# Attention with a squared-ReLU MLP on one core: phases of six and eight score units around one whole product unit

## The chip, the core and the metric

The kernel runs on one core of one Trainium2 chip, as a single program. The metric is the time of one execution in microseconds (us). Engines are named as the profile names them: PE (TensorE; PEld is its weight load), DVE (VectorE), ACT (ScalarE), POOL (GpSimd) and SP (the queue that issues most DMAs). Three timed runs of the kernel before stand at 1247.25, 1248.50 and 1248.59 us, median 1248.5 us.

## The reference

For 2048 positions and width 512, with 32 heads of size 16 that share one key and one value head:

```
x = A_x;  g = sigmoid((x * gate_w).sum(-1))
a = softmax((x@wq) . (x@wk)^T / 4) @ (x@wv)  per head, then @ wo
b = relu(x @ w1 + b1)**2 @ w2 + b2           # F = 1792
out = g * a + (1 - g) * b
```

Everything is float32. Large products are made of rounded parts: a number is split into a rounded part r and a rest l, and r·r + r·l + l·r is summed.

## The kernel before, in words

**Score units.** The heads are worked in 32 groups ("its") of four heads, each with 512 query columns. A group has 32 score units: 128 keys times 256 query columns for all four heads. A unit is two matmuls of 49 rows each, one on the upper and one on the lower half of the PE array's rows, into two PSUM banks (`s`, L730). One exponential of ACT over 128x1024 elements (L734) reads both banks and writes half of an `e` tile in SBUF. There are 1024 units, two buffers of `s` (two banks each) and four `e` tiles (two units each).

**Context.** Later, units are multiplied with the values (`acc`, L745): for two units that share an `e` tile, four matmuls of 512 columns on four column strips of the array.

**Product units.** All other large products (the queries, x·w1, h·w2, the output projection) are units of 9 or 12 terms, some at the end of 3 or 6. A term has 128 rows, and is made as two matmuls of 64 rows: half 0 on the upper rows of the array, half 1 on the lower. `stream` (L188) gives each half a PSUM bank of its own (`mm`, three buffers) and lets half 1 follow half 0 five terms behind (`LAG`). The halves are added by DVE: `first` evicts one bank, `second` the other. A w1 unit (`hidden`, L624) thus takes five DVE instructions: bias (L637), add (L641), squared ReLU (L642), and the split into r and l (L178, L179). An h·w2 unit (`summed`, L646) takes two of L664.

**Phases.** PE's order is written by `phase` (L1002): scores of the coming units, with terms of product units between them (a "slot" is one term of half 0 beside one term of half 1), and then the context of units scored a phase earlier. `plan` (L1028) takes four units with eight slots (a full phase) while product work is ahead, and two units with two or three slots (a light phase) after that. The scores run four or two units ahead of the context.

**The other queues.** DVE also divides the finished contexts in pieces of 86 columns (`divide`, L752: four instructions and an accumulator read, at most one piece a phase), and makes the rests l of weights and inputs (L487, L179); `turn_of_chores` (L606) deals these out by a budget. ACT rounds weights (L491) and copies each finished group's `acc` out (L771). DMAs bring weights, store and load queries and contexts, and store `res`, the MLP's part, to DRAM.

Of the kernel before, what the change touches and what calls it, by code (L numbers as in the profile page):

```python
# [21 lines left out]
KT = D // 128  # L22
# [12 lines left out]
BUDGET = 2.7  # L35
PARTS = [slice(a, min(a + 86, CH)) for a in range(0, CH, 86)]
LANDS = 8.0
GROUPS = (0, 1, 2, 3), (4, 5, 6, 7), (8, 9, 10), (11, 12, 13)
FULL, LIGHT = 4, 2
LAG = 5  # L40
# [25 lines left out]
def exact_shift(tc, k_aug, v_ext, qs, oTs, gms, ress, cs, wo, split, outproj, stream, unpack):  # L66
# [63 lines left out]
    with tc.tile_pool(name="gx", bufs=1) as gx, tc.tile_pool(name="gy", bufs=4, space=PSUM) as gy:  # L130
# [6 lines left out]
        for c in range(NC):  # L137
            oT = gx.tile([128, KT, CH], F32, name="oT")
            orr, orl = [gx.tile([128, KT, CH], F32R, name=n) for n in ("orr", "orl")]
            before = gx.tile([128, KT, CH], F32, name="res")  # L140
            ots = [gx.tile([128, D], F32, name=f"ot{i}") for i in range(2)]
            nc.sync.dma_start(before, ress[c])
            nc.sync.dma_start(oT, oTs[c * NG:c * NG + NG].rearrange("(t u) d n -> (u d) t n", u=2))
            split(orr, orl, oT)
            for _ in stream(outproj(c, before, ots, orr, orl, wor, wol, "gm"), gy):
                pass
# [3 lines left out]
def mix_kernel(ctx: ExitStack, tc: tile.TileContext, xT, wkv, wq, wo, w12, b1, b2, cst, out):  # L150
# [37 lines left out]
    def stream(units, pp):  # L188

        late = []

        def follow(keep):
            if len(late) > keep:
                late.pop(0)()

        for unit in units:
            if unit is None:
                if late:  # L200
                    follow(0)
                    yield 1
                else:
                    yield 0
                continue
            terms, outs, tag = unit
            banks = [pp.tile([128, CH], F32, name=tag)]

            def product(i, half, terms=terms, outs=outs, banks=banks, tag=tag):
                if len(banks) == half:  # L210
                    banks.append(pp.tile([128, CH], F32, name=tag))
                a, b = terms[i]
                rows = slice(64 * half, 64 * half + 64)
                nc.tensor.matmul(banks[half], a[rows], b[rows], start=i == 0, stop=i == len(terms) - 1)  # L214
                if i == len(terms) - 1:
                    outs[half](banks[half])

            for i in range(len(terms)):
                late.append(lambda i=i, p=product: p(i, 1))
                product(i, 0)  # L220
                follow(LAG)
                yield 1
        while late:
            follow(0)
            yield 1

# [5 lines left out]
    def outproj(c, before, ots, orr, orl, wor, wol, tag):  # L232
        for j in range(4):
# [4 lines left out]
            def first(p, s=s, j=j, ot=ot):  # L238
                nc.vector.scalar_tensor_tensor(ot, p, g[:, s:s + 1], before[:, j], op0=OP.mult, op1=OP.add)
# [13 lines left out]
    with fast, tc.tile_pool(name="at", bufs=1) as at, \  # L253
# [352 lines left out]
        def turn_of_chores(slots):  # L606
# [3 lines left out]
            if soon:  # L610
                return soon.pop(0)()
# [498 lines left out]
```

## Time and profile before

| | |
|---|---|
| median of three runs | 1248.5 us |
| span of the profiled execution | 1243.9 us |
| PE busy | 1233.2 us (99%) |
| ACT busy | 1060.3 us (85%), of it 980.3 in the 1024 exponentials |
| DVE busy | 623.1 us (50%) |
| granted TensorE clock | 1.000 |

The span runs from the first to the last instruction of the profiled execution. Its own time is that span and what lies around it at launch and end; the median of the timed runs is 4.6 us above the span. A PE that is busy for 99% has work in flight all the time, since its matmuls overlap; how densely they start is read from the timeline.

### The profile page before, as it was taken

How to read it: one execution, taken by the hardware profiler on the slowest of the kernel's cores; microseconds unless marked ns; L12 is line 12 of the kernel's file. 1: busy time of each engine (PE TensorE's matmuls, PEld its weight loads, DVE VectorE, ACT ScalarE, POOL GpSimd, SP SyncE). 2: the span in 40 equal slices, each digit the busy share in tenths (PEclk: the TensorE clock that was granted, in tenths of full speed). 3: DMA queues.
4: the chain of work that ended last, by engine and by line, in shares of the span. 5: the costliest groups of instructions: out<-in, count | busy, mean ns of one | idle time of the engine just before them, and what ended most of it. 6: DMA issues, size and time to landing. Idle time of an engine off the chain costs nothing.

```text
span 1243.9 us, 24095 instructions
## 1 busy us (share of the span) xinstructions
PE 1233.2 (99%) x9839; PEld 612.5 (49%) x9839; DVE 623.1 (50%) x1246; ACT 1060.3 (85%) x1178; POOL 59.4 (5%) x75
## 2 busy tenths in 40 slices
PE   9999999999999999999999999999999999999997
PEld 4555555555555555555555555555433333343343
DVE  5666665545565542744827365355441454232433
ACT  6888888888888987988988888888899999999985
POOL 1000300000002000000200000002000000000000
PEclk9999999999999999999999999999999999999999
DMA  6334321211232210222202121121110120011101
GB/s 215 101 96 143 105 79 40 82 48 65 69 113 84 75 57 25 82 73 98 72 29 82 65 81 61 56 81 65 56 57 26 35 69 31 31 48 47 44 31 37
DMA packets 44388, 85.57 MB, mean 69 GB/s; under 512 B 10450, under 2 KB 10706, under 8 KB 43760
## 3 DMA queue, kind: packets, MB, share of 16 engines
q1 hardware_dynamic: 37024, 68.27, 17.0%
q0 software_dynamic: 7104, 15.44, 3.7%
q8 instruction: 79, 1.29, 0.4%
q14 instruction: 37, 0.30, 0.1%
q10 hardware_dynamic: 144, 0.26, 0.1%
HBM read 54.68 MB, written 20.97 MB: 61 GB/s over the span
## 4 chain that ended last, share of the span: by engine, by line
PE 96%; ACT 1%; DVE 1%; DMA 0%; issue 0%; SPq 0%; ACTq 0%
PE acc L745 38%; PE mm L214 31%; PE s L730 25%; ACT e L734 1%; PE mm L312 1%; DMA xf<-in_xT 0%; PE mm L186 0%; PE s L322 0%; DVE kmx L334 0%; PE acc L352 0%; ACT w1r L491 0%; PE mm L802 0%; DVE ot L1073 0%; DVE xlagain L179 0%; DVE w1l L487 0%
## 5 line engine op out<-in xcount | busy, mean ns | idle before, releaser
L734 ACT ACTIVATE e<-s 128x1024 f32<-128x1024 f32 x1024 | 980.3, 1023 | 153.5 <-PE s L730 152.0
L745 PE MATMUL acc<-e,v_ext 128*32 128x512 f32 (+1 forms) x4224 | 509.4, 587 | 0.0
L730 PE MATMUL s<-qa,k_aug 49*128 49x512 f32 x2048 | 452.6, 433 | 0.1
L730 PEld LDWEIGHTS s<-qa,k_aug 49*128 49x128 f32 x2048 | 193.7, 183 | 331.8 <-ACT e L734 300.2
L664 DVE SCALAR_TENSOR_TENSOR res<-mm,omg,res 128x512 f32<-128x512 f32 x128 | 95.8, 750 | 252.2 <-PE mm L214 252.2
L214 PE MATMUL mm<-w2r,hr 64*128 64x512 f32 x896 | 212.2, 393 | 1.0 <-DVE big L641 0.6
L745 PEld LDWEIGHTS acc<-e,v_ext 128*32 128x32 f32 x4224 | 102.7, 108 | 208.7 <-issue 202.0
L214 PE MATMUL mm<-w2l,hr 64*128 64x512 f32 x448 | 159.4, 393 | 0.0
L214 PEld LDWEIGHTS mm<-w2r,hr 64*128 64x128 f32 x896 | 129.0, 187 | 18.4 <-DVE res L664 1.2
L214 PEld LDWEIGHTS mm<-w2l,hr 64*128 64x128 f32 x448 | 83.4, 187 | 7.4
L214 PE MATMUL mm<-xragain,w1l 64*128 64x512 f32 x224 | 80.3, 393 | 0.0
L214 PE MATMUL mm<-xr,w1l 64*128 64x512 f32 x224 | 79.4, 393 | 0.0
L214 PE MATMUL mm<-xlagain,w1r 64*128 64x512 f32 x224 | 79.2, 392 | 0.0
L214 PE MATMUL mm<-xragain,w1r 64*128 64x512 f32 x224 | 78.7, 392 | 0.0
L214 PE MATMUL mm<-xl,w1r 64*128 64x512 f32 x224 | 78.5, 391 | 0.0
L214 PE MATMUL mm<-xr,w1r 64*128 64x512 f32 x224 | 77.0, 392 | 0.0
L641 DVE TENSOR_TENSOR big<-big,mm 128x512 f32<-128x512 f32 x56 | 38.5, 687 | 75.0 <-PE mm L214 74.9
L758 DVE RECIPROCAL n<-n 128x86 f32<-128x86 f32 x90 | 61.9, 688 | 3.1
L637 DVE TENSOR_SCALAR big<-mm,b1t 128x512 f32<-128x512 f32 x56 | 42.0, 750 | 39.0 <-PE mm L214 36.9
L214 PEld LDWEIGHTS mm<-xr,w1r 64*128 64x128 f32 x224 | 41.7, 186 | 4.1
L214 PEld LDWEIGHTS mm<-xragain,w1l 64*128 64x128 f32 x224 | 41.7, 186 | 3.9
L214 PEld LDWEIGHTS mm<-xl,w1r 64*128 64x128 f32 x224 | 41.7, 186 | 3.9
(160 smaller groups left out, 1136.8 us busy)
## 6 DMA issues: line engine op xcount, KB each, us to landing
stage<-in_w SPq DMA_DIRECT2D x56, 256.0 KB
qa<-qs SPq DMA_DIRECT2D x186, 64.0 KB
w1f<-in_w SPq DMA_DIRECT2D x28, 256.0 KB
w2f<-in_w SPq DMA_DIRECT2D x28, 256.0 KB
qs<-qr SPq DMA_DIRECT2D x16, 256.0 KB
ress<-res POOLq DMA_DIRECT2D x4, 1024.0 KB, 4.1
qs<-ql POOLq DMA_DIRECT2D x15, 256.0 KB, 8.2
oc<-accs SPq DMA_DIRECT2D x30, 128.0 KB
```

The costliest lines, as they stand in the source:

```text
L214: nc.tensor.matmul(banks[half], a[rows], b[rows], start=i == 0, stop=i == len(terms) - 1)
L312: nc.tensor.matmul(kvq[c][64 * i:64 * i + 64], wkvf[:, k], xf[c, k], start=a == 0, stop=a == 1, skip_group_check=True, tile_position=(0, 6 ...
L637: nc.vector.tensor_scalar(h[0], p, b1t[:, f:f + 1], None, op0=OP.add)
L641: nc.vector.tensor_tensor(h[0], h[0], p, OP.add)
L664: nc.vector.scalar_tensor_tensor(part, p, omg[:, s:s + 1], part, op0=OP.mult, op1=OP.add)
L730: nc.tensor.matmul(s[:, r].rearrange("p (a n) -> p a n", a=2), k_aug[rows, kt * 128:(kt + 1) * 128], qa[it][rows, :, cols], start=True, st ...
L734: nc.scalar.activation(es[u // 2][:, :, mine], s.rearrange("p r (a n) -> p (r a) n", a=2), AF.Exp, scale=SCALE)
L745: nc.tensor.matmul(acc[h * 32:(h + 1) * 32, cols], v_ext[:, kt], es[u // 2][:, h % 2 * 2 + h // 2, mine], start=(kt == 0), stop=(kt == NK ...
L758: nc.vector.reciprocal(n, n)
```

## The change

**One phase, one whole product unit.** `stream`, its lag and `plan` are gone. Each phase now takes one product unit: its half 0 beside half 1 of the unit of the phase before. Both halves accumulate in one bank, so that a unit is evicted once (`done`) at the end of its second phase. A w1 unit takes four DVE instructions in place of five, an h·w2 unit or an output projection one in place of two, a query unit loses a copy and an add.

**Six or eight units.** `block` chooses how many score units go with a product unit: six, or eight where the units left would not stretch, or four and two at the edges. `PLANS` writes out the order for 6 or 8 units with 12 or 9 slots: `S0` is unit 0 on both halves, `M` a slot, `t` a turn of chores, and the list behind it the order of the exponentials. The scores run four units ahead of the context.

**Raw copies.** `mm` keeps two banks; the third becomes a bank of its own, `x`, with one buffer. `02` and `12` in a plan are the halves of unit 2, made one after the other in bank `x`, each copied unchanged to its place in the `e` tile by DVE; ACT then takes this unit's exponential from SBUF in place. A phase of six units copies one unit so, a phase of eight two.

**Buffers.** After the query units a fifth `e` tile is added, in the place of the query weights; `res` has one buffer in place of two. The output projection fetches `res` by rows, a phase ahead. Up to two pieces of the division are put ahead of a phase (`steps_aside(2 if full else 1)`), and chores are dealt out at a phase's start and at its `t`.

```diff
-FULL, LIGHT = 4, 2
-LAG = 5
+AHEAD = 4
+PLANS = {
+    (8, 12): ("S0 M 04 S1 M M M M M S2 M t 14 S3 M M M M 05 M t M S6 M S7 15", (0, 1, 2, 3, 4, 6, 7, 5)),
+    (6, 12): ("S0 M M S1 02 M t M M M M S3 M t 12 M M S4 M M S5", (0, 1, 3, 4, 2, 5)),
...
-            tc.tile_pool(name="mp", bufs=3, space=PSUM) as mp:
+            tc.tile_pool(name="mp", bufs=2, space=PSUM) as mp:
+        def aside():
+            return mp.tile([128, CH], F32, name="x", bufs=1)
...
-            def first(p):
-                nc.vector.tensor_scalar(h[0], p, b1t[:, f:f + 1], None, op0=OP.add)
-
-            def second(p):
+            def done(p):
                 hr, hl = hs[f] = ring[n % 5]
-                nc.vector.tensor_tensor(h[0], h[0], p, OP.add)
-                nc.vector.scalar_tensor_tensor(h[0], h[0], 0.0, h[0], op0=OP.max, op1=OP.mult)
+                nc.vector.tensor_scalar(h[0], p, b1t[:, f:f + 1], 0.0, op0=OP.add, op1=OP.max)
+                nc.vector.tensor_tensor(h[0], h[0], h[0], OP.mult)
                 split(hr, hl, h[0])
...
+        def score_copy(u, r):
+            x = aside()
+            score(u, r, x)
+            nc.vector.tensor_copy(e_half(u)[:, 2 * r:2 * r + 2], x.rearrange("p (a n) -> p a n", a=2))
+            copied[u] = copied.get(u, 0) + 1
...
+            full = slots > 8
+            tick(True)
+            steps_aside(2 if full else 1)
...
+            evicted = before
+            if before:
+                before[1][0](before[2])
+            before = (unit[0], unit[1:], here) if unit else None
...
+                if rest == 8 and not q_over:
+                    return 4
+                if eights[0] and rest % 8 == 0:
+                    return 8
+                return {8: 8, 10: 6}.get(rest, min(rest, 6))
+            return min(rest, 4 if size > 3 else 2)
```

How the program's order moves is shown at three places. The first is PE in a full phase of before, in the first half of the program: scores (`s`), terms of two product units (`mm`), context (`acc`).

```order
L730 MATMUL s<-qa,k_aug 128x512 x2
L214 MATMUL mm<-w2r,hr 128x512
L214 MATMUL mm<-xl_85,w1r 128x512
L214 MATMUL mm<-w2l,hr 128x512
L214 MATMUL mm<-xr_81,w1l 128x512
L214 MATMUL mm<-w2r,hr 128x512
L214 MATMUL mm<-xr_81,w1r 128x512
L730 MATMUL s<-qa,k_aug 128x512 x2
```

Between two scores stand three slots; the phase goes on so to its fourth score and ends in eight matmuls of context. Now the end of an eight-unit phase of the change, from the first half of its last copied unit (`x`) to the next phase's first score:

```order
L724 MATMUL x<-qa,k_aug 128x512
L1067 MATMUL mm<-xr_80,w1l 128x512 x2
L724 MATMUL s<-qa,k_aug 128x512 x4
L724 MATMUL x<-qa,k_aug 128x512
L762 MATMUL acc<-e,v_ext 32x512 x16
L724 MATMUL s<-qa,k_aug 128x512 x2
```

The context has sixteen matmuls in place of eight, and the second use of bank `x` stands right ahead of it, a few matmuls behind the first. The third place is DVE in the change, in a six-unit phase behind a w1 unit: the eviction (L625 to L184), two pieces of a division (L772 to L776, twice), and then the copies out of bank `x` (L738).

```order
L625 TENSOR_SCALAR big<-mm,b1t 128x512
L626 TENSOR_TENSOR big<-big 128x512
L183 CAST hr<-big 128x512
L184 TENSOR_TENSOR hr<-big,hr 128x512
L772 TENSOR_SCALAR n<-lc 128x86
L773 SCALAR_TENSOR_TENSOR lc,ok<-n,lc 128x86
L775 RECIPROCAL n<-n 128x86
L776 TENSOR_TENSOR oc<-oc,n 128x86
...
L738 COPY e<-x 128x2x256
L464 TENSOR_TENSOR w1l<-stage,w1r 128x512
L738 COPY e<-x 128x2x256
```

At the "..." the same four rows of a piece stand once more. Before, one piece stood between two evictions, and no copy for PE behind it.

357 lines of the change are left out of this document (203 added, 154 removed), and 2 rows, old and new, of the table PLANS.

## The prediction

> **What bounds the kernel now.** I read the page's head first, then the chain that ended last, then the timeline of one phase of each kind.
>
> ```profile
> span 1243.9 us, 24095 instructions
> PE 1233.2 (99%) x9839; PEld 612.5 (49%) x9839; DVE 623.1 (50%) x1246; ACT 1060.3 (85%) x1178; POOL 59.4 (5%) x75
> PE 96%; ACT 1%; DVE 1%; DMA 0%; issue 0%; SPq 0%; ACTq 0%
> ```
>
> PE holds 96% of the chain, so what counts is how densely PE's matmuls start. The timeline shows that. First a full phase (columns: start, length, engine, line, what it writes and reads, count, idle time before with its releaser):
>
> ```profile
> 299.61 0.50 PE L730 MATMUL s<-qa,k_aug 49*128 49x512 f32 x2
> 300.24 3.79 ACT L734 ACTIVATE e<-s 128x1024 f32<-128x1024 f32 x4 [1.08 <-PE s L730]
> 300.66 0.40 PE L730 MATMUL s<-qa,k_aug 49*128 49x512 f32 x2
> 300.89 0.39 PE L214 MATMUL mm<-w2l,hr 64*128 64x512 f32 x1
> ...
> 301.33 0.75 DVE L664 SCALAR_TENSOR_TENSOR res<-mm,omg,res 128x512 f32<-128x512 f32 x1 [1.82 <-PE mm L214]
> ...
> 302.23 0.19 PEld L730 LDWEIGHTS s<-qa,k_aug 49*128 49x128 f32 x2 [0.21 <-ACT e L734]
> 302.30 0.43 PE L730 MATMUL s<-qa,k_aug 49*128 49x512 f32 x2
> 302.66 1.92 PE L745 MATMUL acc<-e,v_ext 128*32 128x512 f32 x16
> 304.51 0.50 PE L730 MATMUL s<-qa,k_aug 49*128 49x512 f32 x2
> ```
>
> Then a light phase:
>
> ```profile
> 1003.37 0.50 PE L730 MATMUL s<-qa,k_aug 49*128 49x512 f32 x2
> 1003.97 1.94 ACT L734 ACTIVATE e<-s 128x1024 f32<-128x1024 f32 x2 [0.19 <-PE s L730]
> 1004.18 0.40 PE L730 MATMUL s<-qa,k_aug 49*128 49x512 f32 x2
> 1004.51 1.06 PE L745 MATMUL acc<-e,v_ext 128*32 128x512 f32 x8
> 1005.50 0.50 PE L730 MATMUL s<-qa,k_aug 49*128 49x512 f32 x2
> ```
>
> Call a score pair or a slot a place. From the first score to the last there are 11 places in 2.69 us (299.61 to 302.30) and 3 in 0.81 us: 0.2335 us a place, and 0.11 more behind the first. From the last score to the next phase's first it is 2.21 us with four units of context and 1.32 with two: 0.445 us a unit and 0.43 fixed. A phase of n units and s slots therefore takes **0.31 + 0.2335(n+s) + 0.445n** us: 4.89 full (304.51 - 299.61 = 4.90) and 2.13 light (1005.50 - 1003.37 = 2.13). The 0.31 us is the price of a phase.
>
> The same rows give the waits' small change. Exponentials follow each other every 0.92 us ((3.79 - 1.02)/3) and the first starts 0.6 us behind its score, a later one 0.5. The second ends at 302.18, and the score that needs its buffer starts at 302.30: 0.12 behind. The last product of a half ends at 301.28, and DVE starts at 301.33: 0.05 behind.
>
> **The change on PE alone.** The order of the two programs has 338 phases before (173 full, nearly all others light) and 162 in the change. Of these 70 have six units and 12 slots (7.18 us by the formula), 47 have eight and 12 (8.54), 17 six and 9 (6.48), 8 eight and 9 (7.84), and 18 short ones together 67 us. All 1024 units and all terms stay. 176 phases fewer times 0.31 is 54.6 us less. In 14 phases a unit of 12 terms lies beside one of 9, three terms alone on their half, 1.5 places each: 5 us more. The two phases ahead of the first context get eight more slots and two more units, 2.8 us more, for which the later ones are counted fewer. **PE alone saves 46 us**: 1243.9 - 46 = 1198.
>
> **Where PE now has to wait.** These rows price the new queues:
>
> ```profile
> L410 DVE COPY qf<-mm 128x512 f32<-128x512 f32 x15 | 10.2, 683 | 6.2 <-PE mm L214 6.2
> L637 DVE TENSOR_SCALAR big<-mm,b1t 128x512 f32<-128x512 f32 x56 | 42.0, 750 | 39.0 <-PE mm L214 36.9
> L642 DVE SCALAR_TENSOR_TENSOR big<-big 128x512 f32<-128x512 f32 x56 | 39.2, 699 | 1.9
> L178 DVE CAST hr<-big 128x512 fp32r<-128x512 f32 x56 | 25.3, 451 | 1.9
> L179 DVE TENSOR_TENSOR hr<-big,hr 128x512 fp32r<-128x512 f32 x56 | 39.1, 699 | 1.9
> L755 DVE TENSOR_SCALAR n<-lc 128x86 f32<-128x86 f32 x90 | 17.9, 199 | 9.9 <-DMA lc<-accs 9.4
> L756 DVE SCALAR_TENSOR_TENSOR lc<-n,lc 128x86 f32<-128x86 f32 x90 | 22.4, 249 | 3.1
> L756 DVE DVE_READ_ACCUMULATOR lc<-n,lc 128x1 f32 x90 | 7.5, 83 | 0.0
> L758 DVE RECIPROCAL n<-n 128x86 f32<-128x86 f32 x90 | 61.9, 688 | 3.1
> L759 DVE TENSOR_TENSOR oc<-oc,n 128x86 f32<-128x86 f32 x90 | 22.4, 248 | 3.1
> ```
>
> *Raw copies in eight-unit phases.* Both halves of a copied unit use the one bank `x`. A copy of the same shape out of PSUM took 683 ns (L410; the new copies write SBUF in two strips, which no row shows, so I take this one as it stands). First half: 0.40 of matmul, 0.05 to DVE, 0.68 of copy, about 0.1 back to PE: the second half can start 1.23 us behind the first. Unit 4's halves are eight places apart (1.87 us), no wait. Unit 5's are three (0.70 us): PE stands 0.53 us right ahead of the context, in each of 47 phases, 25 us. Score S7 next to it waits for exponential 3, which ends at 4.66 us of the phase by the 0.92 us pitch; released 0.12 later that is 0.47 late too, but beside the same wait. With 9 slots there are three places more to make up in ACT's chain: S3 would start at 2.21 us and finds exponential 1 done at 2.54 and released 0.12 later, 0.44; S7 then waits 0.48 for exponential 3. 8 times 0.92 is 7 us. Together **32 us**. Below: with a copy as short as the cast of L178 (451 ns, below) S7's wait takes over, 47 times 0.47 and the 7, 29 us. Above, ACT comes in: exponentials 6 and 7 write the `e` tile that the first pair of context reads, so they start 6.5 us into the phase, and three of them end the chain 8.66 us behind its start. One rounding of weights (0.63 us) still fits into the 9.07 us of such a phase, two or three don't. About ten of these phases have two or more: up to 10 us more, not in the sum.
>
> *Four tiles early.* While the query units run there is no fifth `e` tile. In ten six-unit phases two exponentials wait for the phase's context, and the next phase's second score waits for the last of them: 0.5 us each by the same chain, **5 us**. Bounds 0 and 10.
>
> *DVE's line ahead of a copy.* In a six-unit phase the last product starts at 3.86 us, and the eviction can start at 4.3. Behind a w1 unit it takes 0.75 + 0.70 + 0.45 + 0.70 and four gaps of 0.03 (1.9 us in 56), 2.7 us. Two pieces take 2 x 1.47 and their gaps, 3.2. So the first copy of the next phase starts at 4.3 + 5.9 - 7.18 = 3.05 us instead of 1.5, ends at 3.74, and the second half, due at 2.69, waits till 3.85: 1.2 us. Here DVE has 8.1 us of work in a phase of 7.18, so it cannot catch up. The order has 18 such phases: 13 plain, 3 with a split more (0.45 + 0.70, 2.4 us in all) and 2 with a rest of a weight more (0.7, 1.9 in all): 16 + 7 + 4 = **27 us**. Behind an h·w2 unit (0.75 in place of 2.7) the copy starts in time, and the 22 phases of that kind cost nothing. Bounds: 0, if PE's other waits have already put the phase back by as much, and 35, if splits of inputs fall badly.
>
> What leaves DVE (an add of about 0.7 in 56 w1 units, one of two evictions of 0.75 in 64 h·w2 units, with the smaller ones some 100 us) is no gain by itself: DVE has 1% of the chain. What comes are 396 copies, 270 us. The evictions end long before the bank's next use, a whole phase later; cover gone, they would cost their 0.75 us. The loads of `res` by rows are asked for a phase, 7 us, ahead; a load that landed later would cost only the eviction's delay, which has the same cover.
>
> A rule that speaks against the change: ACT's copies are these rows, of SBUF and of PSUM.
>
> ```profile
> L491 ACT ACTIVATE w1r<-w1f 128x512 fp32r<-128x512 f32 x25 | 15.8, 632 | 0.0
> L771 ACT ACTIVATE accs<-acc 128x512 f32<-128x512 f32 x30 | 18.0, 601 | 7.9 <-PE acc L745 6.9
> ```
>
> From SBUF ACT took 31 ns longer, so 198 exponentials from SBUF cost 6 us of ACT's time, under slack in all but the ten phases above: under 1 us. [...]
>
> **The sum.** 1198 + 32 + 5 + 27 = 1262 us of span, and 4.6 us around it as before: **1266 us**, 1.4% slower. The change saves switches and pays them back in waits.
>
> **Rivals.**
> *Faster: the waits hide each other.* If DVE's lateness costs nothing and only the eight-unit phases wait, the span is 1198 + 32 = 1230, the time 1235; if nothing waits, 1203. The mechanism is the saved switch, 0.31 us in each of 176 phases. It decides from where all waits together stay under 46 us, 0.3 us a phase. For it speaks that both engines have slack on average (ACT 1060, DVE some 790 us of 1200); against it that PE takes its matmuls in order, and a score that waits as at 302.23 holds back the context behind it, so that a local lateness is not made good by a mean.
> *ACT becomes the bound.* If exponentials wait for the context's first pair and roundings pile up behind them, an eight-unit phase takes 9.8 us in place of 9.07 in some 25 of 55 phases: 18 us more, 1284. For it: roundings stand at the phase's start, ahead of exponential 0. Against: a six-unit phase has over 1 us of slack and takes up a delay.
> *It doesn't do what it says.* Halves of different units might no longer run beside each other: were each of some 1,700 slots 10% slower, it would cost 40 us, 1306. Against it: before, too, halves of two units lay side by side, at the same pitch.
>
> **How the numbers follow.** Waits as summed (1252 to 1280): 0.50. Waits hide each other, faster: 0.30. ACT bound: 0.12. Pairing lost: 0.03. The rest, 0.05, lies between, near no change. The range 1218 to 1286 takes in the bounds of the three terms (29 to 42, 0 to 10, 0 to 35) but for the last few us of all their upper ends together, and the larger part of the faster case. About 0.2% is what a measurement of this kernel can tell from no change. Faster by more 0.30, within 0.05, slower 0.65.
>
> **What would show it.** Right: six-unit phases near 7.2 us, eight-unit ones near 9.1; PE's second use of bank `x` waiting for DVE's copy by about half a microsecond ahead of the context; phases near 8.4 us where two pieces follow a w1 unit. Wrong: eight-unit phases at 8.5 us, or no waits of PE on L738; or a place that takes more than 0.24 us.

## The result, and the profile after

The changed kernel takes 1313.6 us (median of four runs, 1311.1 to 1315.8) where the kernel before, on the same chip, takes 1248.6: a ratio of **1.053, with a 95% interval of 1.051 to 1.055**. It is slower, as forecast, but by 65 us and not by 17.5, and the time lies outside the range. The profiled execution took 1312.8 us, 1.8 above its span of 1311.0. (The kernel before has the same 1.8 where one execution has both numbers, 1245.65 and 1243.9; the 4.6 us of the forecast compared one execution's span with the median of others.)

The page's head and its chain that ended last, after the change:

```profile
span 1311.0 us, 24220 instructions
PE 1255.7 (96%) x9839; PEld 673.7 (51%) x9839; DVE 760.4 (58%) x1461; ACT 1065.5 (81%) x1193; POOL 58.7 (4%) x75
PE 68%; DVE 12%; ACT 12%; issue 3%; DMA 3%; SPq 1%; ACTq 0%; DVEq 0%
```

PE held 96% of the chain before and holds 68% now; DVE, ACT and DMAs have the rest. In the groups of instructions the raw copies are new, and PE now stands ahead of scores (after the bar: busy time and mean ns; then the idle time before them, and its releaser; the last line is the kernel before):

```profile
L738 DVE COPY e<-x 128x512 f32<-128x512 f32 x396 | 273.5, 691 | 392.4 <-PE x L724 302.8
L724 PE MATMUL s<-qa,k_aug 49*128 49x512 f32 x1652 | 431.6, 437 | 14.2 <-ACT e L751 13.4
L724 PE MATMUL x<-qa,k_aug 49*128 49x512 f32 x396 | 164.5, 415 | 22.2 <-DVE e L738 19.3
L730 PE MATMUL s<-qa,k_aug 49*128 49x512 f32 x2048 | 452.6, 433 | 0.1
```

A wait during which an earlier matmul is still in flight is not idle time (at 203.07 us, below, the 0.43 us stand at the weight load), so these 36 us are less than what the waits cost.

**Where the 67 us of span went.** I took the start of each phase's first score from both traces, and for each phase set its length against the prediction's formula, 0.31 + 0.2335(n+s) + 0.445n. What is above the formula I call the excess.

| us | before | after | difference |
|---|---|---|---|
| up to the first regular phase | 34.7 | 42.9 | +8.2 |
| phases by the formula | 1190.6 | 1132.9 | -57.7 |
| their excess | 7.6 | 124.1 | **+116.5** |
| last phase and end | 11.0 | 11.1 | +0.1 |
| span | 1243.9 | 1311.0 | +67.1 |

So the fewer phases save what they should, and the waits cost nearly twice the 64 us forecast. By kind of phase (numbered from the head, 0), with the excess of the runs told below; e15 is the best combination:

| excess, us | forecast | after | e1 | e2 | e3 | e4 | e5 | e15 |
|---|---|---|---|---|---|---|---|---|
| eight units (54) | 32 | 45.3 | 57.1 | 46.8 | 31.2 | 33.4 | 40.8 | 27.1 |
| phases 1 to 15 | 5 | 14.7 | 16.1 | 13.6 | 13.7 | 16.5 | 16.7 | 12.2 |
| DVE's line (18 phases) | 27 | 23.9 | 9.4 | 26.4 | 24.7 | 32.6 | 17.9 | 2.0 |
| 59, 92, 135 (output projection) | 0 | 12.6 | 12.4 | -0.2 | 12.5 | 11.7 | -0.2 | -0.2 |
| 78 (second load of x) | 0 | 7.8 | 4.2 | 0.2 | 7.1 | 7.8 | 4.7 | 0.2 |
| other phases of six (50) | 0 | 8.5 | 12.8 | 8.8 | 8.6 | 3.1 | 2.1 | 5.1 |
| 142 to 160 (end) | 0 | 11.3 | 12.4 | 11.2 | 11.1 | 11.1 | 10.3 | 11.6 |
| all | 64 | 124.1 | 124.5 | 106.9 | 109.0 | 116.2 | 92.4 | 57.9 |

(The 14 phases with a unit of 12 terms beside one of 9, 5 us in the forecast's part for PE alone, are in the excess here. The profiled execution of e4 took 1309.4 us, 7.5 more than that run's median, so its column is high.)

An eight-unit phase with one rounding of weights ahead of it, in the timeline of the changed kernel:

```profile
197.72 0.50 PE L724 MATMUL s<-qa,k_aug 49*128 49x512 f32 x2
198.11 0.63 ACT L468 ACTIVATE w1r<-stage 128x512 fp32r<-128x512 f32 x1
198.63 3.77 ACT L751 ACTIVATE e<-s 128x1024 f32<-128x1024 f32 x4
...
200.62 0.19 PEld L724 LDWEIGHTS s<-qa,k_aug 49*128 49x128 f32 x2 [0.38 <-ACT e L751]
...
202.32 0.69 DVE L738 COPY e<-x 128x512 f32<-128x512 f32 x1 [0.33 <-PE x L724]
203.07 0.18 PEld L724 LDWEIGHTS x<-qa,k_aug 49*128 49x128 f32 x1 [0.43 <-DVE e L738]
...
204.69 1.94 ACT L751 ACTIVATE e<-s 128x1024 f32<-128x1024 f32 x2 [1.35 <-PE acc L762]
...
207.07 0.50 PE L724 MATMUL s<-qa,k_aug 49*128 49x512 f32 x2
```

It takes 9.35 us, 0.81 over the formula's 8.54. The rounding stands ahead of the first exponential, so the fourth score waits 0.38 us for ACT, and the last raw score another 0.43 for DVE's copy. Without a rounding only one wait of that size is left (0.45 to 0.50 in all), with two roundings it is 1.33, with two and a copy of `acc` 1.81. ACT itself then stands 1.35 us ahead of the seventh exponential, for the context to free an `e` tile.

Phase 78 shows a wait that was not in the sum (DVE in order, PE behind it):

```profile
678.88 0.40 SPq L660 DMA_DIRECT2D stage<-in_xT  x1
683.04 0.43 DVE L183 CAST xragain<-stage 128x512 fp32r<-128x512 f32 x1 [5.00 <-DMA stage<-in_xT]
...
687.07 0.69 DVE L738 COPY e<-x 128x512 f32<-128x512 f32 x1
...
687.81 0.79 PE L724 MATMUL x<-qa,k_aug 49*128 49x512 f32 x1 [4.80 <-DVE e L738]
690.23 4.28 PE L762 MATMUL acc<-e,v_ext 128*32 128x512 f32 x24
```

SP asks for x behind a line of loads of q; DVE stands 5.00 us on it, with two pieces and the copy behind; PE stands 4.80 us. The context behind takes 4.28 us where other phases of six have 2.78. In phase 59 it is the rows of `res`:

```profile
518.21 3.44 SPq L424 DMA_DIRECT2D qa<-qs  x8
521.74 0.35 SPq L205 DMA_DIRECT2D big<-ress  x1
524.71 0.75 DVE L208 SCALAR_TENSOR_TENSOR big<-mm,g,big 128x512 f32<-128x512 f32 x1 [4.86 <-DMA big<-ress]
525.52 0.50 PE L1067 MATMUL mm<-xr,w1r 64*128 64x512 f32 x2 [1.85 <-DVE big L208]
```

Behind the longest stands, in the head and at the end the clock falls. Seven windows of the changed kernel (busy times by engine, then the mean granted clock, the third number from the end):

```profile
28.00:40.00 12.00, 10.65 (x61) 7.97 (x58) 4.06 (x10) 5.51 (x6) 0.00 (x0) 0.72 0.16 50
384.00:392.00 8.00, 6.38 (x39) 2.54 (x39) 4.58 (x10) 3.65 (x4) 0.54 (x1) 0.79 0.43 131
524.00:532.00 8.00, 6.48 (x42) 4.58 (x46) 5.60 (x15) 4.12 (x5) 0.54 (x1) 0.79 0.10 37
684.00:696.00 12.00, 8.19 (x46) 3.69 (x47) 8.62 (x27) 3.84 (x5) 0.00 (x0) 0.72 0.00 1
804.00:812.00 8.00, 6.45 (x42) 4.71 (x46) 2.88 (x4) 3.30 (x4) 0.54 (x1) 0.79 0.21 81
1156.00:1164.00 8.00, 7.10 (x50) 4.73 (x54) 6.20 (x15) 3.96 (x6) 0.54 (x1) 0.79 0.10 36
1304.00:1311.00 7.00, 0.66 (x3) 0.19 (x1) 1.44 (x2) 0.00 (x0) 0.00 (x0) 0.76 0.24 84
```

(1 - clock) x length is 1.7 us in five of them and 3.4 in two: 15.3 us of clock in all, where the kernel before loses 0.5. Of the 20.4 us of phases 59, 78, 92 and 135, 8.5 are clock.

### The profile page after: what moved, and what is told of

Read it like the earlier page. It is cut to its first block, busy times and chain, and to the rows that moved or that the text cites. A ratio compares the mean times of both kernels' runs of the same rounds, so it can differ in the third digit from the quotient of the medians.

```text
span 1311.0 us, 24220 instructions
## 1 busy us (share of the span) xinstructions
PE 1255.7 (96%) x9839; PEld 673.7 (51%) x9839; DVE 760.4 (58%) x1461; ACT 1065.5 (81%) x1193; POOL 58.7 (4%) x75
## 4 chain that ended last, share of the span: by engine, by line
PE 68%; DVE 12%; ACT 12%; issue 3%; DMA 3%; SPq 1%; ACTq 0%; DVEq 0%
PE acc L762 24%; PE mm L1067 23%; PE s L724 14%; ACT e L751 10%; PE x L724 5%; DVE n L775 2%; DVE e L738 2%; SPq L424 1%; DVE lc L773 1%; DVE big L625 1%; DVE big L626 1%; DMA lc<-accs 1%; DMA big<-ress 1%; ACT w2r L468 1%; DVE hr L184 1%
## 5 line engine op out<-in xcount | busy, mean ns | idle before, releaser
L751 ACT ACTIVATE e<-s 128x1024 f32<-128x1024 f32 x826 | 804.4, 1027 | 217.7 <-PE s L724 126.6
L738 DVE COPY e<-x 128x512 f32<-128x512 f32 x396 | 273.5, 691 | 392.4 <-PE x L724 302.8
L762 PE MATMUL acc<-e,v_ext 128*32 128x512 f32 (+1 forms) x4224 | 475.1, 585 | 0.0
L724 PE MATMUL s<-qa,k_aug 49*128 49x512 f32 x1652 | 431.6, 437 | 14.2 <-ACT e L751 13.4
L762 PEld LDWEIGHTS acc<-e,v_ext 128*32 128x32 f32 x4224 | 121.1, 110 | 259.0 <-issue 255.3
L751 ACT ACTIVATE e<-e 128x1024 f32<-128x1024 f32 x198 | 209.9, 1060 | 0.0
L724 PE MATMUL x<-qa,k_aug 49*128 49x512 f32 x396 | 164.5, 415 | 22.2 <-DVE e L738 19.3
L1067 PE MATMUL mm<-w2l,hr 64*128 64x512 f32 x448 | 135.4, 395 | 0.0
L724 PEld LDWEIGHTS x<-qa,k_aug 49*128 49x128 f32 x396 | 74.4, 188 | 54.0 <-DVE e L738 41.3
L648 DVE SCALAR_TENSOR_TENSOR res<-mm,omg,res 128x512 f32<-128x512 f32 x64 | 47.8, 746 | 14.1 <-PE mm L1067 13.9
L625 DVE TENSOR_SCALAR big<-mm,b1t 128x512 f32<-128x512 f32 x56 | 41.8, 746 | 9.8 <-PE mm L1067 9.8
```

What stands on the lines that cost most here:

```text
L625: nc.vector.tensor_scalar(h[0], p, b1t[:, f:f + 1], 0.0, op0=OP.add, op1=OP.max)
L648: nc.vector.scalar_tensor_tensor(part, p, omg[:, s:s + 1], part, op0=OP.mult, op1=OP.add)
L724: nc.tensor.matmul(dst.rearrange("p (a n) -> p a n", a=2), k_aug[rows, kt * 128:(kt + 1) * 128], qa[it][rows, :, q * HC:q * HC + HC], star ...
L738: nc.vector.tensor_copy(e_half(u)[:, 2 * r:2 * r + 2], x.rearrange("p (a n) -> p a n", a=2))
L751: nc.scalar.activation(e_half(u), src, AF.Exp, scale=SCALE)
L762: nc.tensor.matmul(acc[h * 32:(h + 1) * 32, cols], v_ext[:, kt], es[u // 2][:, h % 2 * 2 + h // 2, mine], start=(kt == 0), stop=(kt == NK ...
```

## The experiments

Each run's "before" is the kernel before on the same chip (medians 1245.9 to 1247.2 us); for each ratio its 95% interval stands behind it. The changed kernel itself was timed beside a kernel before of 1248.6, so a difference in us from its 1313.6 is good to about 3 us. The theory: PE loses the time in order, at bank `x` (DVE's copies) and at scores (ACT's exponentials). The rivals: ACT's amount of work is the bound; late DMAs are; the saved changes between scores and context are not real.

**e1, pieces behind the copies**: the call goes from a phase's start to its end.

```diff
-            steps_aside(2 if full else 1)
...
             exps(todo)
             assert not todo
+            steps_aside(2 if full else 1)
```

> The division pieces are issued behind a phase's last raw copy instead of at the phase's start; their number stays. DVE's line (my theory): the 18 phases in which pieces or evictions stand ahead of a copy carry 23.9 us over the formula in the profile of after; they fall to 0 to 5, and the time by 18 to 24 us, to 1290 to 1296 us. If ScalarE sets these phases instead: the pieces' place does not matter, and the time stays within 4 us of 1313.6. If DVE has no slack behind the copies: the evictions come late, TensorE waits at the product's bank instead, and the gain is under 10 us.

1313.7 us, 1.054 [1.051, 1.056]: no change. The 18 phases do fall, from 23.9 to 9.4 us, but eight-unit phases rise by 11.8, since pieces and a long eviction now stand ahead of the next phase's first copy. The line was moved, not shortened: the last of the three cases. In phase 81 it met POOL's work:

```profile
704.92 6.35 POOL L645 TENSOR_SCALAR res<-big,omg 128x512 f32<-128x512 f32 x4
```
```profile
704.75 1.42 DVE L626 TENSOR_TENSOR big<-big 128x512 f32<-128x512 f32 x1
706.20 2.11 DVE L183 CAST hr<-big 128x512 fp32r<-128x512 f32 x1
708.34 1.05 DVE L184 TENSOR_TENSOR hr<-big,hr 128x512 fp32r<-128x512 f32 x1
709.32 0.68 DVE L738 COPY e<-x 128x512 f32<-128x512 f32 x1
```

Beside it DVE's multiply took 1.42 us (0.69 elsewhere) and its cast 2.11 (0.43), while the copy out of PSUM kept its 0.68.

**e2, two kinds of load on POOL's queue.**

```diff
-                nc.sync.dma_start(ot, ress[c][:, j])
+                nc.gpsimd.dma_start(ot, ress[c][:, j])
...
-                nc.sync.dma_start(stage()[:, :2], xT[c, 2 * a:2 * a + 2].rearrange("k p s -> p k s"))
+                nc.gpsimd.dma_start(stage()[:, :2], xT[c, 2 * a:2 * a + 2].rearrange("k p s -> p k s"))
```

> Two kinds of load, the 128-row pieces of the MLP's result for the output projection and the second loads of x, are issued from POOL's queue instead of SP's. Queue theory (SP's line of eight loads of q and the stores ahead makes them land late, and DVE stands in order behind them): phases 59, 92 and 135 (3.6, 5.3 and 3.8 us over the formula) and phase 78 (7.8 us) fall below 1 us each, the slow matmuls behind them (0.43 us apart) go, and the time falls by 15 to 20 us, to 1293 to 1299 us. If the loads themselves take that long wherever they are issued: within 4 us of 1313.6.

1299.9 us, 1.042 [1.039, 1.045]. The four phases fall from 20.4 us to 0: the queue theory holds for them. The gain is 13.6 and not 20, because phase 68 rose by 3.2 (granted clock 0.50 from 608 to 612 us, as in e3) and the head by 3.0.

**e3, a plan with as many places as slots.**

```diff
-    (8, 12): ("S0 M 04 S1 M M M M M S2 M t 14 S3 M M M M 05 M t M S6 M S7 15", (0, 1, 2, 3, 4, 6, 7, 5)),
+    (8, 12): ("S0 04 S1 M M M M M 14 S2 M M t M S3 05 M M M t S6 M S7 15", (0, 1, 2, 3, 4, 6, 7, 5)),
```

> The plan of the 41 phases of eight units and 12 slots is rewritten with 12 product places (it has 14, of which the last two stay empty, so that only three places lie between the third and the fourth raw copy): copies 6 places apart, the fourth score one place later. My theory (TensorE waits in order at the bank of the raw copies, 0.43 us, and for exponentials, 0.38 us, in each): their excess falls from 32.6 us to 8 to 16, the time to 1290 to 1299 us. If ScalarE's own work sets these phases: what is no longer waited for at the raw copy is waited for at a score, and the time falls by under 6 us.

1298.8 us, 1.043 [1.041, 1.044]: 14.7 us, as the theory has it. The 41 phases fall from 32.6 to 19.4 us; without a rounding 0.15 is left of 0.46. The trace holds a second lesson, in phase 68. PE waits there as in the changed kernel, 1.96 us, but now the clock falls:

```profile
593.40:599.00 5.60, 3.64 (x31) 2.67 (x28) 4.58 (x13) 3.64 (x5) 0.00 (x0) 0.99 0.48 140
599.00:602.00 3.00, 3.00 (x12) 1.63 (x14) 1.52 (x4) 1.64 (x2) 0.00 (x0) 0.50 0.27 87
602.00:606.20 4.20, 4.20 (x24) 0.79 (x16) 3.92 (x12) 2.28 (x4) 0.00 (x0) 0.56 0.01 4
606.20:610.00 3.80, 3.80 (x34) 2.89 (x30) 3.04 (x6) 2.94 (x4) 0.00 (x0) 1.00 0.11 31
```

The phase is 5.9 us over the formula in place of 2.7. The same wait (1.95 us) left the clock at 1.00 in the changed kernel's trace (600 to 612 us); the last section shows where the two differ.

**e4, roundings on VectorE.**

```diff
-                    w_round(half, scalar_copy)
+                    w_round(half, nc.vector.tensor_copy)
```

> The rounding of the weights (0.63 us on ScalarE between two phases) is done by VectorE at the same place of the program. If ScalarE's line sets the phases of eight units: those with one rounding ahead fall from 0.80 to about 0.47 us over the formula, those with two from 1.33 to 0.47, six-unit phases behind two roundings from 0.83 to 0.2: together 12 to 20 us, to 1294 to 1302 us. If it is VectorE's line and the raw copy's bank: the rounding now stands ahead of the phase's first raw copy, and the time stays within 6 us or grows.

1301.9 us, 1.045 [1.043, 1.046]. Phases with roundings fall as forecast (eight units -11.9, other phases of six -5.4), and DVE's line pays 8.7 of it back. So a rounding's place in ACT's line costs, as does its place in DVE's.

**e5, ScalarE's extra work where ScalarE waits.** Roundings go to a plan's last `t`, and the copy of `acc` (`finish`) behind the next phase's first exponentials.

```diff
+                    if i == last_tick:
+                        rounds()
+                if i == 7:
+                    closes()
...
-            for half in halves():
-                if not soon and w_ready(half):
-                    w_round(half, scalar_copy)
...
-                finish(it, acc)
+                closing.append((it, acc))
```

> ScalarE keeps its roundings of weights and its copies of accs, but takes them in the middle of a phase, where it waits for an e tile (1.35 us ahead of the seventh exponential of an eight-unit phase), instead of ahead of the phase's first exponential. If it is the place in ScalarE's line that costs (a late first exponential, for which TensorE waits at the fourth score): phases of eight with one, two and two roundings and a copy fall from 0.80, 1.33 and 1.81 us over the formula to about 0.46, six-unit phases behind such lines from 0.83 to 1.18 to about 0.2, together 14 to 22 us, to 1292 to 1300 us. If ScalarE's amount of work bounds these phases: under 5 us.

1284.1 us, 1.030 [1.027, 1.033]: 29.5 us, more than expected. ACT does as much as before, so its amount of work was not the bound. But half of the fall in the excess (31.7 us) has another cause: 15.9 is in phases 59, 78, 92 and 135. The eight-unit phases gave 4.5, less than in e3 and e4, since phases 16, 33, 62, 81 and 109 rose by 7.3. The timeline of ACT, where the rounding now lies in the wait for the `e` tile:

```profile
192.43 1.06 ACT L751 ACTIVATE e<-e 128x1024 f32<-128x1024 f32 x1
193.38 0.63 ACT L468 ACTIVATE w1r<-stage 128x512 fp32r<-128x512 f32 x1
194.54 1.94 ACT L751 ACTIVATE e<-s 128x1024 f32<-128x1024 f32 x2 [0.54 <-PE acc L762]
```

Such phases are 0.46 over the formula. The surplus is the output projection (12.6 us to 0), which I had not expected: SP's stores of `accs` no longer stand ahead of the loads of q, so in the phases before 59, 92 and 135 these start 3.0 to 4.4 us ahead of the phase and not 2.2 to 2.7 us into it, and `res` lands in time.

**e7, one more change from context to scores and back in each phase.** A score nobody reads is put into the middle of the context of 135 phases.

```diff
+                context(acc, range(u, u + m - 4))
+                it2, kt2, q2 = place(u)
+                nc.tensor.matmul(aside()[:, :CH].rearrange("p (a n) -> p a n", a=2), k_aug[:KR, kt2 * 128:(kt2 + 1) * 128],
+                                 qa[it2][:KR, :, q2 * HC:q2 * HC + HC], start=True, stop=True)
+                context(acc, range(u + m - 4, u + m))
```

> A score nobody reads (on the raw copies' bank while it is free) stands in the middle of the context of each phase of six or eight units with 9 or 12 slots, about 130 of them: work of 0.2335 us and one more change from context to scores and back. If such a change costs the 0.31 us that the formula gives a phase: 0.54 us in each, 60 to 72 us in all, 1374 to 1386 us. If the 0.31 us is not the change but something at a phase's edge: 0.23 us each, 1340 to 1345 us. If the time is hidden behind ScalarE: under 20 us.

1351.8 us, 1.085 [1.083, 1.087]: +38, between the forecasts, since only part of the phases pay. PE's timeline in a plain phase of six:

```profile
301.73 0.50 PE L724 MATMUL s<-qa,k_aug 49*128 49x512 f32 x2
...
306.15 1.07 PE L762 MATMUL acc<-e,v_ext 128*32 128x512 f32 x8
307.15 0.50 PE L1136 MATMUL x<-qa,k_aug 49*128 49x512 f32 x1
307.58 1.92 PE L762 MATMUL acc<-e,v_ext 128*32 128x512 f32 x16
309.43 0.50 PE L724 MATMUL s<-qa,k_aug 49*128 49x512 f32 x2
```

It takes 7.70 us, 0.57 more than without. Less the score's 0.2335, a change there and back costs 0.33 us: the formula's 0.31 is real. It also shows who sets each phase. Of the 126 phases from 16 to 141, 66 grew by 0.50 to 0.62 us (PE sets them), 33 by nothing (all but two or three of DVE's 18 among them), 20 by 0.15 to 0.4 (ACT holds them from a point on); the other seven moved with late loads and the clock, by -2.6 to +3.2.

**e8, no raw copies**: the four plans with all scores through `s`.

```diff
+    (8, 12): ("S0 M S1 M M t S2 M M S3 M M S4 M M t S5 M S6 M M S7", (0, 1, 2, 3, 4, 5, 6, 7)),
+    (6, 12): ("S0 M M S1 M t M M M S2 M M S3 M t M S4 M M S5", (0, 1, 2, 3, 4, 5)),
```

> The plans of phases of six and eight units without raw copies: all scores go through the two s banks. If the copies hide exponentials that TensorE would otherwise wait for in order (the last score of six needs the fourth exponential: 0.5 + 4 x 1.0 us, then 2.7 us of context and 0.3; of eight the sixth): six-unit phases come to about 7.8 us, eight-unit ones to about 10.9, less the 24 us of DVE's line: 1400 to 1440 us. If the copies' bank and VectorE's line cost more than they give: below 1313 us.

1371.4 us, 1.100 [1.098, 1.102], 58 us above the changed kernel: 10.3 us a phase of eight and 7.6 most of those of six, below my figures (I had taken ACT's pitch as 1.0 us, not 0.92) but far above 1313. The copies give more than they cost.

**Together: e6, e9 to e15.** e6 joins e1, e2, e3 and e5 and a like plan for nine slots.

> All together: loads on POOL's queue, both plans of eight-unit phases with as many product places as slots and the copies apart, the division pieces behind the last raw copy, ScalarE's roundings and accs copies in the middle of a phase. If the waits add up as in the single runs (13.6 from the loads, 14.8 from the plan, some 4 from the plan of nine slots, about 15 from ScalarE's line, 0 to 14 from the pieces): 1250 to 1268 us, level with or up to 2% above the kernel before. If they cover one another, so that one removed wait uncovers the next: above 1280 us.

1283.0 us, 1.030 [1.028, 1.032], no better than e5: the rival's case, waits that cover one another. In the new plan the last `t` falls behind the seventh unit's score, so the rounding misses ACT's wait; and two pieces with a long eviction stand ahead of a copy. e9 puts the `t` ahead of that score, in the plan of nine slots too, and gives the copy of `acc` to DVE behind a phase's first raw copy (here e6 against e9).

```diff
-    (8, 12): ("S0 04 S1 M M M M M 14 S2 M M t M S3 05 M M M t S6 M S7 15", (0, 1, 2, 3, 4, 6, 7, 5)),
+    (8, 12): ("S0 04 S1 M M M M M 14 S2 M t M M S3 05 t M M M S6 M S7 15", (0, 1, 2, 3, 4, 6, 7, 5)),
...
-            nc.scalar.activation(a, acc, AF.Copy)
+            if soon:
+                nc.scalar.activation(a, acc, AF.Copy)
+            else:
+                nc.vector.tensor_copy(a, acc)
```

> The combination with three repairs of what its trace showed: the rounding stands ahead of the seventh unit's score, not behind it, so that it falls into ScalarE's wait for an e tile (0.96 us); the copy of accs is VectorE's, behind the phase's first raw copy; in the first phases (up to 15) the accs copy stays where it was (there its delay cost 5 us at phases 13 and 14, where scores waited 5.4 us). If the excesses over the formula are separate waits: early 18.9 to 14, eight-unit phases with 12 slots 26.4 to 10, the other eight-unit ones 14.5 to 8, six-unit ones 9.7 to 4, the rest as it was: about 60 us are left of 92, and the time is 1247 to 1260 us. If ScalarE's work or the e tiles set the eight-unit phases whatever its order: above 1270 us.

1265.9 us, 1.016 [1.014, 1.017], above the forecast 1247 to 1260. Eight-unit phases behave (26.4 to 18.3 for those of 12 slots); the early ones don't, since ACT stands on a weight that an earlier rounding wants too soon:

```profile
142.28 0.63 ACT L468 ACTIVATE w2r<-w2f 128x512 fp32r<-128x512 f32 x1 [6.53 <-DMA w2f<-in_w]
```

On e9, e10 drops the two phases of delay behind a pass and lets two pieces follow in phases of eight, one in others.

```diff
-            for _ in range(2):
-                yield
...
-            steps_aside(2 if full else 1)
+            steps_aside(2 if n > 6 else 1)
```

> The second combination, and the division pieces follow a pass at once, one behind a six-unit phase's last raw copy and two behind an eight-unit phase's, instead of two in each phase with two phases left empty first. DVE's line (a piece takes 1.5 us, an eviction with its rounding 2.8): the excess left in the phases of pieces and evictions (10 us) goes to 2 to 5, and the time is 5 to 9 us below that of the second combination. If the pieces now wait for the landing of the pass's result, VectorE stands in line and the time is the same or above.

1291.4 us, 1.038 [1.033, 1.043]: the wrong way. DVE stands on the landing of `lc`, PE at bank `mm` behind it (up to 6.0 us, at phase 13). e11 sets `LANDS`, the planner's time for a weight to land, higher on e9.

```diff
-LANDS = 6.0
+LANDS = 10.0
```

> The second combination with LANDS at 10 instead of 6: a weight's rounding is given to ScalarE at the earliest 10 us after its load was asked for. In the second combination's trace ScalarE stood 6.5 us on a load of w2f at phase 13 (asked for at 133.9, rounded at 142.3) with the exponentials behind it, and TensorE 5.4 us on a score. If that wait is the load's: the early phases and phase 16 fall from 22 to about 14 us over the formula, and the half clock behind them (some 2 us) goes: 7 to 11 us, to 1255 to 1259 us. If later roundings push VectorE's remainders and the products that need the weights: the same or above 1266.

1263.3 us, 1.012 [1.007, 1.018], above the forecast 1255 to 1259. ACT's wait is gone, but phases 14 and 16 stand 7.5 and 4.5 us over the formula, so the early phases gain only 2.6. On e11, e12 puts one piece beside a long eviction, two beside others, a phase after the pass; pieces that are left over go ahead of the next pass's copy.

```diff
-            for _ in range(2):
-                yield
+            yield
...
-            steps_aside(2 if full else 1)
+            long = before is not None and "hidden" in before[1][0].__qualname__
+            steps_aside(1 if long or not full else 2)
```

> As the one with LANDS at 10, and the division pieces start one phase after their pass and come one at a time in a phase whose eviction is the long one with the rounding (2.8 us), two in the others. VectorE's line: what is left at phases 25, 33, 41 to 43, 50, 62, 81, 109 and 126 (1.2 to 2.3 us each, 15 us) falls to 3 to 8 us, and the time is 7 to 12 us below the run with LANDS alone, level with the kernel before within 0.5%. If pieces that are left over at the next pass's end are then done in a lump ahead of its accs copy: no gain, or a loss.

1257.9 us, 1.009 [1.006, 1.012]: 5.4 us where 7 to 12 were expected. DVE's line falls from 10.5 to 2.0 us; at phase 13 a piece comes in the phase of its own pass's copy:

```profile
134.37 0.21 DVE L772 TENSOR_SCALAR n<-lc 128x86 f32<-128x86 f32 x1 [5.99 <-DMA lc<-accs]
```

e13 forbids that, with a phase more of delay for the first passes; e14 takes the delay back; e15 takes two lumps of pieces apart (here e12 against e15).

```diff
+                fresh.append(True)
...
-            long = before is not None and "hidden" in before[1][0].__qualname__
-            steps_aside(1 if long or not full else 2)
+            long = before is not None and any(w in before[1][0].__qualname__ for w in ("hidden", "ready"))
+            steps_aside(1 if long or not full or fresh and n < 8 else 2)
+            fresh.clear()
```

> As the third combination, and a pass's division pieces never start in the phase in which its result is copied out (in its trace VectorE stands 6.0 us on the landing of lc at phase 13, and about 1 us at phases 30, 59, 87, 97, 106 and 135, with TensorE waiting behind it at the product's bank); the first four passes wait one phase more. If the saved changes of mode reach the end once the waits are gone: 8 to 15 us less than the third combination's 1257.9, 1243 to 1250 us, level with the kernel before or up to 0.3% below it. If the pieces then pile up ahead of the next accs copy, or another wait takes their place: 1254 or above.

1254.5 us, 1.006 [1.004, 1.007]: above the forecast 1243 to 1250, where the rival had it.

> As the fourth combination, without the extra phase for the first four passes: there it only pushed pieces together (5.8 us at phase 25, 4.3 at phase 16, each with half clock behind). If waits are all that is left: phase 16 at about 1.5 us, phase 25 at 0.4, phase 13 below 1, so some 9 us less over the formula than the fourth combination (65 us), and 2 us of clock: 1243 to 1248 us, level with the kernel before within 0.3%. If it stays at 1253 or above, something else than these waits keeps it there.

1250.6 us, 1.004 [1.002, 1.005]: lower, but above the forecast 1243 to 1248.

> As the fifth combination, with its two lumps of pieces taken apart: at phase 16 the first MLP eviction was not counted as a long one (two pieces and 3.9 us of other VectorE work stand ahead of the phase's first copy: 6.0 us over the formula, and half clock), and in eight-unit phases two pieces may follow in the phase in which the pass's result is copied out (its landing then lies inside the phase), so that none are left for the next pass's start (phases 25, 63, 82, 83: 1.0 to 1.8 us). If waits are all that is left: 8 to 10 us less over the formula than 60.6, and up to 2 us of clock: 1239 to 1246 us, level with the kernel before or up to 0.6% below it. If other waits take the place: 1249 or above.

1250.1 us, **1.003 [1.002, 1.004]**; runs from 1246.5 to 1253.4. e15 is level with e14 within their spread and above the forecast 1239 to 1246: where two waits went, others remained. From e9 on, the interval of each step but e10 overlaps that of the step before it; which wait went is read from the traces. The chain of e15:

```profile
PE 85%; DVE 8%; ACT 4%; DMA 1%; issue 1%; SPq 0%; ACTq 0%; DVEq 0%
```

PE has 85% of the chain again, and the excess is 57.9 us of 124.1. Nothing but the order and place of the same work, and the queue of some loads, was changed, and of the 5.3% all but 0.3% came back. No version here beats the kernel before.

**e16 and e17, the head.** The first regular phase starts at 42.4 to 43.0 us in six traces of the combinations and at 46.8 and 46.9 in two (e13, e15), the latter with half clock from about 25.5 to 43 us. Twins were put beside the first twelve lone products, in e16 on e15, in e17 on the changed kernel.

```diff
+                if r and before is None:
+                    a, b = unit[0][done[1]]
+                    nc.tensor.matmul(aside(), a[64:128], b[64:128], start=True, stop=True)
+                    done[1] += 1
+                    return
```

> As the sixth combination, and the twelve first-half products of the very first phase, which run alone on 64 of TensorE's 128 rows, get a twin beside them on the other 64 rows (the same operands' other half, into the raw copies' bank, read by nobody). In its trace and in others the clock granted falls to half at 24 to 31 us, in or right behind these products, for 3.4 or some 14 us; in the kernel before, whose products there run in pairs, it does not. If the lone half rows are why the clock falls: the clock stays at 1.00 there, the next phase begins 4 to 8 us earlier than in the sixth combination's trace (at 39 to 42 instead of 46.9 us), and the median is 2 to 5 us lower: 1245 to 1248 us, level with the kernel before. If it is the wait of 1.4 us behind them: the clock falls all the same and the time is within 2 us of 1250.

> The changed kernel with nothing but these twelve twins: the head's share of the loss. If the lone half rows let the clock fall: the first regular phase begins 2 to 3 us before 42.9, and the time is 1308 to 1312 us; else 1313 within 2.

1260.2 us, 1.011 [1.009, 1.013], and 1322.7 us, 1.062 [1.061, 1.064]: both slower than without twins, against both forecasts. The twins did not start with their products but 0.23 to 0.56 us behind them (the first to the last of the twelve started in 5.8 us in e16, 25.57 to 31.33, and in 3.4 in the changed kernel, 26.17 to 29.53), and the same code put twins into phase 143 too (9.2 and 5.3 us over the formula). And the clock fell in e17 before most of the products had run:

```profile
22.00:26.00 4.00, 3.79 (x33) 3.12 (x33) 3.38 (x8) 2.96 (x6) 0.00 (x0) 0.97 0.22 47
26.00:30.00 4.00, 3.89 (x14) 1.45 (x12) 1.81 (x3) 2.05 (x2) 0.00 (x0) 0.50 0.36 124
```

So lone half rows are not shown to be the cause. Why the clock falls in the head of every changed kernel (to 0.50 for 3.4 to 20.5 us, between 24 and 47 us) and not in the kernel before (1.00 there) stays open.

## Why the prediction was wrong, point by point

The direction was right and the mechanism in the main; what failed is the sum of the waits. The excess is 60 us above the forecast 64: 20.4 in the phases that wait for loads, 13.3 in eight-unit phases, 9.7 in the first 15, 11.3 at the end, 8.5 in other phases of six, less 3.1 in DVE's line. The signs named in advance came: plain phases of six take 7.1 us, eight-unit ones 9.0 and more, and PE waits about half a microsecond at its second use of bank `x`.

- **PE alone.** "PE alone saves 46 us": by the formula 57.7, less 8.2 in the head, where 2.8 was forecast, and 4.9 in the unequal phases: 44.6. The agreement is in part luck, since 57.7 stands for 54.6 and the head's 8.2 holds waits and 3.4 us of clock. e7 confirms the price of a phase by another way.
- **DVE's line ahead of a copy**, 27 us: 23.9. The mechanism was right; the size hides two errors that cancel. The 13 plain phases cost 11.4 and not 16, the other five 12.4 and not 11, of which 1.7 is clock in phase 42. e1 showed that moving the line does not remove it; e12 removed it by spreading the pieces.
- **Raw copies in eight-unit phases, 32 us: a step that failed**, with 45.3. The wait at bank `x` was there, 0.43 us (0.53 forecast). But "One rounding of weights ... still fits" does not hold: a late first exponential makes the *fourth score* wait 0.38 us, and this adds to the wait at `x` and does not run beside it. I had timed ACT's chain by its end and not by its start. In the 41 such phases of 12 slots e3, e4 and e5 took 13.2, 10.6 and 5.4 us of that away; the up to 10 us "not in the sum" belonged in it.
- **"The loads of res ... would cost only the eviction's delay, which has the same cover": the step that failed by most**, a term put at nothing: 12.6 us, and with phase 78's load of x, in no term at all, 20.4. The cover was a phase for PE's bank, but DVE works in order: what stands behind a late landing is the next raw copy, and PE waits for that (4.80 us in phase 78) or for its product bank (1.85 in phase 59). e2 and e5 each took the 12.6 away, by the queue and by the queue's order.
- **Four tiles early**, 5 us: 14.7 for all the first 15 phases. Their other waits (ACT's line, splits of x ahead of a copy, up to 2.5 us each at 13 to 15) were not looked at; nor was the end, 11.3. No run here takes these apart.
- **The clock** was in no term: 15.3 us of it are lost in the changed kernel, part of the excess above and of the head's. In e3 the phase with a wait of 1.96 us stood 5.9 us over the formula with half clock behind the wait, and 2.7 without.
- **The rivals.** ACT as the bound: not by its amount (e3, which left it, took 13.2 us out of 41 phases), but roundings at a phase's start, which the rival named, did cost. Waits that hide each other: not in the changed kernel, whose waits cost more than their sum. In the combinations one removed wait did uncover another (e6, e13 and e15 came out where that rival had them). Pairing lost: no, plain phases of six run at the formula to 0.1 us.
- **What stays open**: e15's 57.9 us, among them 11.6 at the end, 12.2 in the first 15 phases and 8.0 in the eight phases of nine slots; and the head.

## What to carry to other kernels

Slack on average was no cover for engines that work in order: DVE was busy for 58% of the changed kernel's span and ACT for 81%, and its phases stood 124.1 us over the formula. When a copy that TensorE needs is put on VectorE or an exponential on ScalarE, list everything that stands ahead of it in that queue, each with the landing it waits for, and ask for the worst phase. Extra work can go into the place where its engine already waits for something else (e5) or to another engine (e4); in both runs a part came back as a wait in another line, and e5's larger gain was half due to the order of its loads. And price a stand of TensorE with what its clock does after it (8.5 of the 20.4 us of phases 59, 78, 92 and 135).

## What the runs showed of the hardware that was not expected

- **Half clock after a window of little work.** A wait of 1.96 us in e3 was followed by a granted clock of 0.50, and places came every 0.43 us in place of 0.2335; an equal wait in the changed kernel (1.95 us) was not. The clock records in the traces show where the two differ. In the changed kernel half clock lasts 3.41 or 6.83 us (the last stretch is cut off by the end) and its stretches begin whole multiples of 3.413 us apart (from 386.10 to 526.05 us are 41 of them, to 1157.52 us 226). I cut the 18 traces of the changed kernel and its variants into these windows, without their first 45 us and without windows that were at half clock already. Where PE was busy for less than 50% of a window, half clock followed in 59 of 60; where for more than 60%, in 2 of 6366; between, in 9 of 38; in the changed kernel's own trace in 4 of 4, 0 of 355 and 1 of 3. The wait in e3 lies in one window (first line), the equal one in the changed kernel begins late in one (last line) and ends in the next:

```profile
595.43:598.84 3.41, 1.45 (x13) 0.89 (x10) 3.24 (x9) 1.61 (x2) 0.00 (x0) 1.00 0.31 85
601.15:604.56 3.41, 3.41 (x32) 1.39 (x26) 2.45 (x5) 3.41 (x6) 0.00 (x0) 1.00 0.50 98
604.56:607.97 3.41, 2.06 (x17) 1.33 (x14) 3.17 (x12) 2.57 (x3) 0.00 (x0) 1.00 0.60 200
```

PE (first number behind the length) is busy for 1.45 us of 3.41 there and for 2.06 here. No run set this share on purpose, so that it is the cause is not shown, and it does not explain the head: in the changed kernel PE was busy throughout the window before half clock at 31.12 us (3.41 of 3.41 us).
- **VectorE beside GpSimd.** While POOL's four operations ran (e1, 6.35 us from 704.92 us on), DVE's multiply of SBUF by SBUF took 1.42 us for 0.69 and its cast from SBUF 2.11 for 0.43; the copy out of PSUM kept its 0.68. The rows show these operations slowed while both engines were at work, and not by what.
- **An exponential in place in SBUF** takes 1060 ns where one from PSUM takes 1027, 33 ns more; the prediction's row gave 31:

```profile
L751 ACT ACTIVATE e<-s 128x1024 f32<-128x1024 f32 x826 | 804.4, 1027 | 217.7 <-PE s L724 126.6
L751 ACT ACTIVATE e<-e 128x1024 f32<-128x1024 f32 x198 | 209.9, 1060 | 0.0
```
